# Loading the first FFN weights in pieces of the contraction, with six PSUM banks open at once for the first row tile

## The chip, the cores and the metric

The kernel runs on one core of a Trainium2 chip. The metric is the device time of one execution in microseconds (us). The profile's "span", from the first to the last instruction, is about 1.8 us shorter than that time.

## The reference, cut to what matters

A layernorm of `x` (2048 rows of 640) feeds a SwiGLU feed-forward network and an attention over the last 512 cached keys of 32 heads. Only the start of the feed-forward part is touched by the change:

```python
xn = layernorm(x)                    # 2048 x 640
g = silu(xn @ w_gate)                # 640 x 1536
u = xn @ w_up                        # 640 x 1536
ffn = (g * u) @ w_down
out = x + attention(xn) * silu(ffn)
```

## The kernel before

The rows are handled in tiles of 128. The first four row tiles go through the first three column blocks of the hidden layer one at a time, as soon as their data is there; everything after that uses matmuls of 512 columns. The first columns of both weight matrices (384 columns, 480 KB each) are loaded whole, between the first row tiles of `x`. SP and ACT name the issuing queues of SyncE and ScalarE.

```python
load_x(0)                       # halves: one by SP, one by ACT
load_x(1, nc.scalar)
load_gu(0, nc.scalar)           # gate by SP, up by ACT, all 5 chunks of the contraction
load_x(2); load_x(3)            # SP
load_gu(1)
# ... cut: x tiles 4 to 7, the other weights

def ln_stats(t, between=None):  # VectorE: two bn_stats, between() after the first, bn_aggr
def ln_sqrt(t):                 # ScalarE: Sqrt of the variance
def ln_apply(t):                # VectorE: reciprocal, then (x - mean) * rstd -> xn
def ready(t):
    ln_transpose(t)             # TensorE: 5 transposes of xn into PSUM
    # ... cut: ScalarE (tile 0: part by VectorE) copies them to xnT
    if t < 3:
        ln_sqrt(t + 1)
    if t == 2:
        nc.scalar.activation(act_t[:], one_t[:], ACT.Silu)   # loads the Silu table early

ln_stats(0); ln_sqrt(0)
ln_stats(1, lambda: ln_apply(0))
ready(0)
keep_warm(4)                    # matmuls on zeros
for t in range(4):
    rows = slice(t * P, (t + 1) * P)
    order = [(f, s) for s in range(2) for f in range(3)]      # s: 0 gate, 1 up
    for k, (f, s) in enumerate(order if t == 0 else sorted(order)):
        if k == 4 and t < 3:
            if t < 2:
                ln_stats(t + 2, lambda: ln_apply(t + 1))
            else:
                ln_apply(t + 1)
            ready(t + 1)
        hidden_mm(first[f][s][:, rows], s, f, rows)           # 5 matmuls, one per chunk c
        # ... cut: gates in tile 3
```

The softmax here doesn't subtract the row's maximum and nothing guards it: scores larger than these inputs give would overflow.

## Time and profile before

| | before |
|---|---|
| time, median of 6 runs | 930.38 us (930.01 to 930.88) |
| span of the profiled run | 928.8 us |
| TensorE (PE) busy | 920.7 us, 99% of the span |
| first hidden matmul | 7.66 us |
| first matmul of row tiles 1, 2, 3 | 10.70, 13.04, 15.38 us |
| first 512-column matmul | 17.05 us |

These are lines of the page of the kernel before. They are the span, the busy time of each engine, and the start of the chain that ended last with its shares by engine.

```profile
span 928.8 us, 18808 instructions
PE 920.7 (99%) x8026; PEld 578.7 (62%) x8026; DVE 579.7 (62%) x846; ACT 476.2 (51%) x849; POOL 65.1 (7%) x57
PE 98%; DMA 1%; DVE 1%; ACT 0%; issue 0%; SPq 0%; DVEq 0%
```

TensorE is busy nearly throughout, so only its idle time can be won. The Trainium skill ("Perfetto Trace Analysis", section "Identifying the Most-Contended Engine") warns that matmul busy time is no measure of distance to the roofline. Here it is used for something else: to see where TensorE waits. Those waits sit at the start, as the table by windows of the kernel before shows. Its columns are the stretch and its length, then busy time and instruction count of PE, weight loads (PEld), DVE, ACT and POOL, then clock, DMA share and GB/s.

```profile
0.00:17.05 17.05, 14.05 (x156) 9.76 (x157) 7.42 (x25) 7.26 (x14) 0.79 (x8) 1.00 0.93 280
17.05:928.00 910.95, 906.63 (x7874) 568.95 (x7871) 572.25 (x822) 468.96 (x836) 64.29 (x49) 1.00 0.38 79
```

Of the first 17.05 us TensorE idles 3.00 (17.05 - 14.05). The next two fences are from the timeline of the kernel before. The columns are start, duration of the group, engine, line, operation, output and inputs, shapes, count, and in brackets the idle time before it and what ended it. First TensorE:

```profile
7.66 0.73 PE L271 MATMUL sc<-xnT,wg_sb 128*128 128x128 bf16 x10 [0.58 <-DMA wg_sb<-in_B_w_gate_dram]
9.47 0.45 PE L259 MATMUL tp<-ident,xn 128*128 128x128 bf16 x5 [0.52 <-DVE xn L248]
10.70 0.44 PE L271 MATMUL sc<-xnT,wg_sb 128*128 128x128 bf16 x5 [0.22 <-ACT xnT L321]
```

Then VectorE (DVE):

```profile
8.37 0.49 DVE L225 BATCH_NORM_STATS2 stats<-x_t 128x6 f32<-128x320 bf16 x1 [1.32 <-DMA x_t<-in_A_x_dram]
8.78 0.15 DVE L247 RECIPROCAL rstd<-rstd 128x1 f32<-128x1 f32 x1
8.96 0.45 DVE L248 TENSOR_SCALAR xn<-x_t,mv,rstd 128x640 bf16<-128x640 bf16 x1
```

The statistics at 8.37 are those of x tile 2. They wait 1.32 us for their DMA. The reciprocal and the `TENSOR_SCALAR` behind them make xn of row tile 1, which needs nothing of x tile 2; it is only queued behind. TensorE's transposes of tile 1 at 9.47 wait for that xn. In the chain of waits of the kernel before this DMA is the one large early piece (columns: start, length, what):

```profile
2.24 6.11 DMA x_t<-in_A_x_dram
8.37 0.49 DVE stats L225
```

### The profile page before, as it was taken

The numbers are of one execution on the slowest core, as the hardware profiler recorded it, in microseconds if no ns is written. First come the engines' busy times: TensorE is split into PE (matmuls) and PEld (weight loads), VectorE is DVE, ScalarE is ACT, GpSimd is POOL, SyncE is SP. The second block draws the span as 40 slices with busy tenths as digits, with TensorE's granted clock in tenths as the row PEclk, the third lists the DMA queues.
The fourth block names the chain that finished last, engine by engine and source line by source line (L and its number), as shares of the span: only waits on it lengthen the run. The fifth ranks groups of instructions, "written<-read, shape, count | busy, mean of one in ns | idle before, by whom it ended". The sixth has DMA issues, their size and how long they took to land.

```text
span 928.8 us, 18808 instructions
## 1 busy us (share of the span) xinstructions
PE 920.7 (99%) x8026; PEld 578.7 (62%) x8026; DVE 579.7 (62%) x846; ACT 476.2 (51%) x849; POOL 65.1 (7%) x57
## 2 busy tenths in 40 slices
PE   8999999999999999999999999999999999999997
PEld 5455555574847475757575757575666666666675
DVE  5433321467676767676766667676767676767656
ACT  3222222556565656565555555555555555656561
POOL 0000000000000000000000000000000000003975
PEclk9999999999999999999999999999999999999999
DMA  9321510053535343343434342525252616262523
GB/s 299 69 43 44 114 35 1 1 80 85 93 71 87 77 80 84 73 91 73 91 69 95 60 104 56 108 52 112 41 123 38 126 35 129 34 144 61 147 59 107
DMA packets 240084, 76.34 MB, mean 82 GB/s; under 512 B 221056, under 2 KB 240000, under 8 KB 240000
## 3 DMA queue, kind: packets, MB, share of 16 engines
q1 hardware_dynamic: 239120, 74.40, 38.1%
q8 instruction: 63, 1.03, 0.5%
q10 hardware_dynamic: 880, 0.74, 0.3%
q14 instruction: 21, 0.17, 0.1%
HBM read 39.45 MB, written 2.62 MB: 45 GB/s over the span
## 4 chain that ended last, share of the span: by engine, by line
PE 98%; DMA 1%; DVE 1%; ACT 0%; issue 0%; SPq 0%; DVEq 0%
PE sc L497 22%; PE mm L414 22%; PE mm L450 18%; PE sc L428 18%; PE sc L271 10%; PE mm L293 6%; DMA x_t<-in_A_x_dram 1%; PE sc L450 1%; PE mm L306 0%; PE mm L271 0%; ACT xnT L321 0%; DVE s_f L540 0%; PE mm L428 0%; ACT L327 0%; DVE ob L538 0%
## 5 line engine op out<-in xcount | busy, mean ns | idle before, releaser
L432 ACT ACTIVATE p_t<-sc 128x1024 bf16<-128x1024 f32 x254 | 253.1, 1023 | 136.4 <-PE sc L428 136.4
L419 DVE TENSOR_REDUCE qT<-mm 128x512 bf16<-128x1024 f32 x189 | 231.3, 1224 | 104.0 <-PE mm L414 101.5
L467 ACT ACTIVATE O_b<-mm,r 128x192 bf16<-128x192 f32 x484 | 164.5, 422 | 175.2 <-DVE r L456 97.6
L414 PE MATMUL mm<-xnT,wq_p 64*128 64x512 bf16 x1890 | 235.0, 376 | 0.0
L497 PE MATMUL sc<-wo_p,OT_b 128*128 128x320 bf16 x1482 | 223.4, 299 | 0.0
L512 DVE TENSOR_TENSOR sacc<-sacc,sc 128x640 f32<-128x640 f32 x216 | 176.7, 821 | 60.9 <-PE sc L497 60.9
L428 PE MATMUL sc<-qT,khat 64*128 64x512 bf16 x1524 | 195.5, 376 | 0.0
L450 PE MATMUL mm<-V_p,p_t 128*128 128x193 bf16 x1984 | 185.8, 246 | 0.0
L450 PEld LDWEIGHTS <-p_t 128*128 128x128 bf16 x2048 | 173.1, 97 | 14.9 <-issue 7.0
L497 PEld LDWEIGHTS <-OT_b 128*128 128x128 bf16 x1488 | 143.5, 98 | 47.3
L414 PEld LDWEIGHTS <-wq_p 64*128 64x128 bf16 x1890 | 90.7, 94 | 112.4 <-issue 4.2
L428 PEld LDWEIGHTS <-khat 64*128 64x128 bf16 x1536 | 74.8, 94 | 91.0
L279 DVE TENSOR_TENSOR hT<-sc,sg 128x512 bf16<-128x512 f32 x46 | 31.7, 692 | 85.8 <-ACT sg L278 85.8
L515 POOL TENSOR_TENSOR sacc<-sacc,g_76 128x640 f32<-128x640 f32 x16 | 22.1, 1402 | 757.8 <-ACT O_b L467 757.8
L456 DVE RECIPROCAL r<-mm 128x4 f32<-128x4 f32 x124 | 22.7, 183 | 73.1 <-PE mm L450 68.9
L278 ACT ACTIVATE sg<-sc 128x512 bf16<-128x512 f32 x46 | 27.4, 597 | 73.2 <-PE sc L271 71.6
L271 PE MATMUL sc<-xnT,wg_sb 128*128 128x512 bf16 (+1 forms) x260 | 58.0, 354 | 1.2 <-ACT xnT L321 0.7
L271 PE MATMUL sc<-xnT,wu_sb 128*128 128x512 bf16 (+1 forms) x260 | 58.2, 354 | 0.0
L293 PE MATMUL mm<-wd_sb,hT 128*128 128x320 bf16 x384 | 56.6, 299 | 0.0
L293 PEld LDWEIGHTS <-hT 128*128 128x128 bf16 x384 | 37.6, 98 | 18.9
L271 PEld LDWEIGHTS <-wu_sb 128*128 128x128 bf16 x285 | 25.8, 98 | 26.5
L271 PEld LDWEIGHTS <-wg_sb 128*128 128x128 bf16 x285 | 25.8, 98 | 24.7 <-DMA wg_sb<-in_B_w_gate_dram 1.1
(63 smaller groups left out, 250.5 us busy)
## 6 DMA issues: line engine op xcount, KB each, us to landing
wo_p<-in_A_wo_dram SPq DMA_DIRECT2D x16, 480.0 KB, 4.3
K_p<-in_A_k_cache_dram SPq DMA_DIRECT2D x32, 192.0 KB, 3.3
V_p<-in_A_v_cache_dram SPq DMA_DIRECT2D x32, 192.0 KB, 3.1
wq_p<-in_A_wq_dram SPq DMA_DIRECT2D x64, 80.0 KB, 3.1
wq_p<-in_A_wq_dram SPq DMA_DIRECT2D x16, 160.0 KB, 3.3
x_r<-in_A_x_dram SPq DMA_DIRECT2D x16, 160.0 KB, 4.1
x_t<-in_A_x_dram SPq DMA_DIRECT2D x14, 160.0 KB, 3.1
wg_sb<-in_B_w_gate_dram SPq DMA_DIRECT2D x4, 480.0 KB, 6.7
```

The source lines that it names most:

```text
L271: nc.tensor.matmul(out, w_sb[:, c, f * P : (f + 1) * P], xnT[:, c, qc], start=(c == 0), stop=(c == NC - 1),)
L278: nc.scalar.activation(sg[:], g, ACT.Silu)
L279: nc.vector.tensor_tensor(hTs[b][:, f, :], u, sg[:], ALU.mult)
L293: nc.tensor.matmul(dn[:, 0:HD], hTs[b][:, f, ti * P : (ti + 1) * P], wd_sb[:, f, cols], start=(f == 0), stop=(f == NF - 1),)
L414: nc.tensor.matmul(q_ps[:, h, :], pairs[pr]["wq"][r, c, j * P : (j + 1) * P], xnT[r, c, b * 512 : (b + 1) * 512], start=(c == 0), stop=(c ...
L419: nc.vector.reduce_sum(qTs[i][:, j, :], q_ps[:, :, :].rearrange("p h n -> p n h"), axis=AX.X)
L428: nc.tensor.matmul(sc[:, h, :], khat[r, j, ks], qT[r, j, :], start=(j == 0), stop=(j == 2))
L432: nc.scalar.activation(p_t[:, :, :], sc[:, :, :], ACT.Exp, scale=scale)
L450: nc.tensor.matmul(acc[:, k, h * 256 : h * 256 + Dh + 1], Ps[i][kc][:, h, qt * P : (qt + 1) * P], V_p[:, kc, h, 0 : Dh + 1], start=(kc == ...
L467: nc.scalar.activation(O_b[:, qt, h, :], a_k[:, h, 0:Dh], ACT.Copy, scale=r[:, k, h, :])
L497: nc.tensor.matmul(ps, OTs[i][:, 3 * qt + j, :], pairs[i // NB]["wo"][:, j, n * HD : (n + 1) * HD], start=(first and j == 0), stop=(end an ...
L512: nc.vector.tensor_tensor(s_t, s_t, sc[:, :, 0:HD], ALU.add)
```

## The change

The intent is to let TensorE begin on row tile 0 when the first chunk of the contraction has landed, instead of waiting for a whole matrix. The first gate and up weights are each loaded as three DMAs (1, 2 and 2 chunks of 128 rows). The contraction is the sum over the 640 features of a row, five chunks of 128. Row tile 0 runs chunk by chunk over all six accumulators, so six banks of PSUM, the memory in which TensorE accumulates, are open at once. The diff does more than its title says: it also takes the statistics of x tile 2 out of the way of tile 1's normalization, places the next tile's transposes after three of six groups instead of four, moves the Silu table load behind tile 3's copy, and drops one of the warm-up matmuls.

```diff
-        load_gu(0, nc.scalar)
+        for cs in (slice(0, 1), slice(1, 3), slice(3, NC)):
+            for eng, w_sb, w in ((nc.sync, wg_sb, B_w_gate), (nc.scalar, wu_sb, B_w_up)):
+                src = w[cs.start * P : cs.stop * P, 0:FQ].rearrange("(c p) f -> p c f", p=P)
+                eng.dma_start(out=w_sb[:, cs, 0:FQ], in_=src)
         load_x(2)
         load_x(3)
 ...                                              # hidden_mm takes the chunks to do, cs
         def ready(t):
 ...
-            if t < 3:
-                ln_sqrt(t + 1)
-            if t == 2:
-                nc.scalar.activation(act_t[:], one_t[:], ACT.Silu)
 ...
         ready(0)
-        keep_warm(4)
+        ln_sqrt(1)
+        keep_warm(3)
+        banks = [(f, s) for f in range(3) for s in range(2)]
         for t in range(4):
-            order = [(f, s) for s in range(2) for f in range(3)]
-            for k, (f, s) in enumerate(order if t == 0 else sorted(order)):
-                if k == 4 and t < 3:
-                    if t < 2:
-                        ln_stats(t + 2, lambda: ln_apply(t + 1))
+            order = [(*fs, [c]) for c in range(NC) for fs in banks]
+            if t:
+                order = [(*fs, range(NC)) for fs in banks]
+            for k, (f, s, cs) in enumerate(order):
+                if k == len(order) * 3 // 5 and t < 3:
+                    if t == 1:
+                        ln_stats(3, lambda: ln_apply(2))
                     else:
                         ln_apply(t + 1)
                     ready(t + 1)
-                hidden_mm(first[f][s][:, rows], s, f, rows)
+                    if t == 0:
+                        ln_stats(2)
+                    if t < 2:
+                        ln_sqrt(t + 2)
+                    else:
+                        nc.scalar.activation(act_t[:], one_t[:], ACT.Silu)
+                hidden_mm(first[f][s][:, rows], s, f, rows, cs)
```

More of the change, by code (lines that the diff above doesn't have):

```diff
@@ L186, in load_x, with load_gu @@
                 eng.dma_start(out=x_t[t][:], in_=x2[t * P : (t + 1) * P, :])
-        def load_gu(q, eng=nc.sync):
+        def load_gu(q):
             cols = slice(q * FQ, (q + 1) * FQ)
@@ L192, in load_gu @@
             )
-            eng.dma_start(
+            nc.sync.dma_start(
                 out=wu_sb[:, :, cols], in_=B_w_up[:, cols].rearrange("(c p) f -> p c f", p=P)
@@ L266, with hidden_mm @@
         hTs = {}
-        def hidden_mm(out, s, f, qc):
+        def hidden_mm(out, s, f, qc, cs=range(NC)):
             w_sb = (wg_sb, wu_sb)[s]
-            for c in range(NC):
+            for c in cs:
                 nc.tensor.matmul(
@@ L319, in ready @@
             ln_transpose(t)
-            rows, n = slice(t * P, (t + 1) * P), 3 if t == 0 else NC
+            rows = slice(t * P, (t + 1) * P)
+            n = NC if t else 3
             nc.scalar.copy(xnT[:, 0:n, rows], tps[t][:, 0:n, :])
```

## The prediction

> **What bounds the kernel now.** The page gives PE 920.7 us busy of 928.8 us (99%); the chain that ended last is 98% PE. The change touches only the time before the first 512-column matmul (17.05 us in the timeline); from there to 40 us PE is busy 22.95 of 22.95 us (table by windows). So only PE's idle time before 17 us can be won, and a gain there should shift everything behind it.
>
> **That stretch before (timeline, waits, chain).** 120 hidden matmuls and 15 transposes from 7.66 to 17.05 us, at 0.28 us per five: 7.6 us of work in 9.4 us. Losses:
> - PE waits 0.58 us for the first gate weights (7.08 to 7.66).
> - Tile 1's transposes start at 9.47 (0.52 us idle): its xn is computed on VectorE behind a stats instruction that waits for x tile 2 (it begins at 8.37). This DMA is the chain's largest early piece (6.1 us).
> - From a tile's transposes to the next tile's first matmul pass 1.23 us (transposes, 0.69 us copy); only two groups (0.56 us) fill it; tiles cost 2.34 us each (10.70, 13.04, 15.38).
> - The table load (1.28 us) stands before tile 3's copy.
>
> **What changes.**
> 1. Weights in three pieces per matrix, contraction-major order; same bytes and queue order. X tile 2 and the last up piece should land near 8.3 as now, the first pieces near 5 to 6, the middle near 7.3 (estimate from the DMA view's bytes per us, landing about 1 us after the bytes). PE starts near 7.1 and does 18 of 30 matmuls before the last pieces.
> 2. Tile 1's normalization no longer waits for x tile 2: transposes near 8.15.
> 3. Transposes after 3 of 6 groups instead of 4: a tile costs about 2.1 us (0.84 + 1.23).
> 4. The Silu table load moves behind tile 3's copy; the gates start near 15.5 (16.13 now), early enough.
> 5. Cost: four more DMA issues of 0.45 to 0.6 us, two on ScalarE's queue ahead of the Sqrt table load (2.43 to about 3.5), so the first Sqrt slips 0.3 us (4.69 to 5.0), and tile 0's copies with it. The Trainium skill, "DMA: Bandwidth & Descriptors", section "Rules for kernel authors", says that issuing engines share the same 16 DMA engines; the overlapping landings here agree, so I count no bandwidth gain.
>
> **Sum.** Tile 0 starts at 7.1, tile 1 9.4, tile 2 11.9 (held by x tile 2's statistics), tile 3 14.1, first 512-column matmul 15.8 instead of 17.05. All 1.2 us lie on the critical path: 930.39 - 1.2 = 929.2 us.
>
> **Range** 928.4 to 930.1. Within 2% is practically certain: all idle before 17 us is under 4 us.
>
> **What shows each step.** Timeline: first hidden matmul near 7.1, released by the xnT copy, not the weights; tile 1's transposes near 8.2, before x tile 2's stats end; tile starts as above; Sqrt table load near 3.5; at most about 0.4 us gap before tile 2's transposes. PE's busy total nearly unchanged, its idle 1.2 us less.
>
> **What would make it wrong.** Issue on ScalarE slower than 0.6 us each: every 0.1 us delays tile 0. Pieces landing late through uneven sharing between the queues: tile 0 stalls within the contraction. A later clock rise (the warm-up matmuls take 427 ns each until about 6 us): up to 1 us. The late table load delaying the first gate until a PSUM bank is missing: I expect over 1 us of slack.

## The result, and the profile after

The changed kernel takes 929.82 us (median of 6 runs, 929.58 to 929.89) against 930.38 us: a gain of 0.56 us. A later set of five runs gave 929.95 against 930.45, a gain of 0.50 us. The ratio is 0.9993 with a 95% interval of 0.998 to 1.0006. Ratios here are the mean time of one kernel's fast runs over that of the other's in the same rounds, so they are not quite the ratio of the medians. By this measure the two kernels are the same; the traces and the experiments are needed to say more. In the first set all six runs of the changed kernel (929.89 at most) lie below all six of the kernel before (930.01 at least); in the later set the ranges overlap.

The page after, the lines that answer to those of before:

```profile
span 927.8 us, 18795 instructions
PE 919.5 (99%) x8009; PEld 578.7 (62%) x8025; DVE 579.4 (62%) x846; ACT 475.5 (51%) x849; POOL 65.0 (7%) x57
```

In this trace the span is 1.0 us shorter. The busy total of PE fell by 1.2 us, but it is of little use here: 17 fewer matmul records are in it, while the change removes one matmul. The table by windows, cut at the first 512-column matmul of the kernel after, is clearer:

```profile
0.00:16.00 16.00, 13.77 (x155) 9.78 (x156) 7.17 (x24) 6.60 (x13) 0.79 (x8) 1.00 0.91 278
```

TensorE idles 2.23 us there (16.00 - 13.77) instead of 3.00. The 1.05 us by which the 512-column matmuls start earlier are 0.77 us of idle time and 0.28 us of work, about the one warm-up matmul. The timeline of TensorE after:

```profile
7.06 0.22 PE L274 MATMUL sc<-xnT,wg_sb 128*128 128x128 bf16 x1
8.09 0.44 PE L262 MATMUL tp<-ident,xn 128*128 128x128 bf16 x5
9.31 0.44 PE L274 MATMUL sc<-xnT,wg_sb 128*128 128x128 bf16 x5
10.98 0.45 PE L262 MATMUL tp<-ident,xn 128*128 128x128 bf16 x5 [0.67 <-DVE xn L251]
16.00 0.38 PE L274 MATMUL mm<-xnT,wg_sb 128*128 128x512 bf16 x1
```

Tile 0 starts at 7.06 without a wait, tile 1's transposes come at 8.09 instead of 9.47, and tile 1 starts at 9.31 instead of 10.70: 1.39 us won. Then a new wait stands at 10.98, where the transposes of tile 2 wait 0.67 us for their xn. The timeline of VectorE after shows why:

```profile
7.44 0.45 DVE L251 TENSOR_SCALAR xn<-x_t,mv,rstd 128x640 bf16<-128x640 bf16 x1
8.79 0.89 DVE L228 BATCH_NORM_STATS2 stats<-x_t 128x6 f32<-128x320 bf16 x2 [0.90 <-DMA x_t<-in_A_x_dram]
10.48 0.45 DVE L251 TENSOR_SCALAR xn<-x_t,mv,rstd 128x640 bf16<-128x640 bf16 x1
```

Tile 1's xn (7.44) is no longer behind the statistics of x tile 2. But x tile 2 lands at 8.76 now, 0.4 us later than in the trace of before, and from there its statistics, its square root and its xn (10.48) set the pace. Tiles 1 to 2 take 2.90 us instead of 2.34, tiles 2 to 3 take 2.12 instead of 2.34. The sum is -1.39 + 0.56 - 0.22 = -1.05 us. The chain of waits after agrees; the same DMA is still its large early piece, but now it leads to tile 2:

```profile
3.42 5.34 DMA x_t<-in_A_x_dram
8.79 0.90 DVE stats L228 x2
```

**Does a gain at the start reach the end?** Yes, and completely. For all 14 traces (two of the kernel before, two of the changed one, ten of other versions) the span is the start of the first 512-column matmul plus 911.75 to 911.91 us. That start ranges from 15.62 to 17.73 us. So nothing is given back later, and a difference in time is a difference before about 17 us. It also means that single traces scatter: the second trace of the changed kernel has that start at 16.31 instead of 16.00, and medians of several runs are needed for the size of an effect.

**From x tile 2 to the 512-column matmuls.** The table of the experiments below allows one more difference: the start of the first 512-column matmul minus the start of x tile 2's statistics. It is 8.67 to 8.68 us in both traces of the kernel before and in e2 (old order of VectorE's work), 8.23 in e8 (only the wait put back), and 7.21 to 7.23 in both traces of the changed kernel, both of e1, in e9 and in e10. So the new order shortens the path behind x tile 2 by 1.46 us, 1.02 us of it by the one move that e8 undoes; how late x tile 2 lands then adds to the time. In e3, e5 and e7 (7.50, 7.87, 8.02) a weight load that TensorE waits for in tile 0 is what holds instead; in e4 (7.39) the table load adds 0.18.

### The profile page after: what moved, and what is told of

Its sections match the earlier page's. It is cut to its first block, busy times and chain, and to the rows that moved or that the text cites. A ratio compares the mean times of both kernels' runs of the same rounds, so it can differ in the third digit from the quotient of the medians.

```text
span 927.8 us, 18795 instructions
## 1 busy us (share of the span) xinstructions
PE 919.5 (99%) x8009; PEld 578.7 (62%) x8025; DVE 579.4 (62%) x846; ACT 475.5 (51%) x849; POOL 65.0 (7%) x57
## 4 chain that ended last, share of the span: by engine, by line
PE 98%; DMA 1%; DVE 1%; issue 0%; DVEq 0%
PE sc L508 22%; PE mm L425 22%; PE mm L461 18%; PE sc L439 18%; PE sc L274 10%; PE mm L296 6%; DMA x_t<-in_A_x_dram 1%; PE sc L461 1%; PE mm L274 0%; PE mm L309 0%; DVE s_f L551 0%; PE mm L439 0%; DVE stats L228 0%; DVE ob L549 0%; DVE s_f L548 0%
```

## The experiments

Theory A: the gain comes from taking tile 1's normalization off the wait for x tile 2, with a smaller part from the earlier transposes; the pieces themselves add nothing and make x tile 2 land later. Theory B, the change's own intent: the pieces and the contraction-major order bring the gain. The expectations call them by these letters. Each kernel was run on the same chip as runs of the kernel before; all gave correct results. The edits below are cut, and are against the changed kernel; only that of e2 is against the kernel before. "Start" is the start of the first 512-column matmul in the one profiled run.

| version | time, median (range) | minus before, same chip | start | x tile 2's statistics begin |
|---|---|---|---|---|
| before_again | 930.72 (930.09 to 930.99) | +0.18 | 17.07 | 8.40 |
| after_again | 929.95 (929.33 to 930.27) | -0.50 | 16.31 | 9.10 |
| e1_reorder_only | 928.99 (928.90 to 930.16) | -1.46 | 16.59 | 9.38 |
| e1_again | 929.03 (928.92 to 929.32) | -1.51 | 15.62 | 8.39 |
| e2_pieces_only | 930.86 (930.59 to 931.39) | +0.41 | 17.73 | 9.06 |
| e3_x2_early | 929.39 (928.86 to 929.60) | -1.06 | 15.77 | 8.27 |
| e4_table_before_copy | 929.86 (929.76 to 930.28) | -0.68 | 16.60 | 9.21 |
| e5_after_four | 930.25 (929.94 to 930.79) | -0.34 | 16.70 | 8.83 |
| e7_gates_both | 929.15 (928.48 to 929.39) | -1.39 | 15.69 | 7.67 |
| e8_wait_back | 930.57 (930.32 to 930.96) | -0.02 | 17.34 | 9.11 |
| e9_issue_late | 929.38 (929.26 to 930.54) | -1.21 | 15.69 | 8.48 |
| e10_x2_behind_ups | 929.47 (929.03 to 930.39) | -1.12 | 16.62 | 9.40 |

The intervals of the ratios are about 0.0012 wide to each side, or 1.1 us. The single runs say more: all five runs of e1_again, for example, lie below every run of the kernel before on that chip (929.32 at most against 930.09 at least).

### after_again and before_again: both kernels once more

No edit.

> The changed kernel once more, as the yardstick of the runs beside it. Both theories: the trace repeats (tile 0's first hidden matmul 7.1 us, tile 1's 9.3, tile 2's 12.2, tile 3's 14.3, first 512-column matmul 16.0). If the 1.05 us that the first trace shows before 17 us survive to the end, the timed gain over the kernel before is about 1.0 us (929.4); if some of it is given back later, about 0.5 us.

> The kernel before itself, for a second trace. The six traces so far agree that the span is the start of the first 512-column matmul plus 911.8 us (911.75 to 911.83), so the spread of the times (930.0 to 931.0) should be the spread of that start. Theory A and B alike: the start is near 16.8 (from the median time) rather than the 17.05 of the first trace, the sum holds again within 0.1 us, and x tile 2 and the whole gate weights land at times that differ by some tenths of a us from the first trace though the bytes moved by 7 us are the same.

The gain of after_again was 0.50 us, as in the first set, so the expectation's alternative "some of it is given back later" had the right number for the wrong reason. The sum of start and 911.8 us held. The first pair of traces had simply caught a slow run of the kernel before (930.71 us) and a quick one of the changed kernel (929.60). The trace of before_again was again one with a start of 17.07, and not the 16.8 that the median suggests. Its landings did not scatter as expected: its gates landed at 7.64 and x tile 2 at 8.38, as in the first trace.

### e1_reorder_only and e1_again: the reordering without the pieces

```diff
-        for cs in (slice(0, 1), slice(1, 3), slice(3, NC)):   # six DMAs
+        for eng, w_sb, w in ((nc.sync, wg_sb, B_w_gate), (nc.scalar, wu_sb, B_w_up)):
+            src = w[:, 0:FQ].rearrange("(c p) f -> p c f", p=P)
+            eng.dma_start(out=w_sb[:, :, 0:FQ], in_=src)
-            order = [(*fs, [c]) for c in range(NC) for fs in banks]
+            order = [(f, s, range(NC)) for s in range(2) for f in range(3)]
```

> The changed kernel with the first weights loaded whole and gates before ups in tile 0, as before; the reordering of VectorE and ScalarE work and the transposes after 3 of 6 groups stay. Theory A (the gain comes from taking tile 1's normalization off the wait for x tile 2 and from earlier transposes; the pieces add nothing and make x tile 2 land later): x tile 2 lands near 8.35 again, tile 0 starts 7.66, tile 1 9.7, tile 2 11.9, tile 3 14.1, first 512-column matmul 15.8, so 0.2 us EARLIER than the changed kernel. Theory B (the pieces and the contraction-major order bring the gain): first 512-column matmul at 16.5 or later, since PE again waits 0.58 us for whole weights.

> The reordering without the pieces once more: the profiled run of the first time was the slowest of its five (930.16 against 928.9 to 929.7), with gates landing at 8.42. Theory A: the median is again near 929.0, 0.8 us below the changed kernel's 929.8; if the profiled run is a quick one, gates land near 7.6, tile 0 starts near 7.5, tile 2's transposes wait little and the first 512-column matmul starts near 15.4. Theory B (the pieces help, the first median was luck): median near 930.

Without the pieces the kernel is faster still: 928.99 and 929.03 us, a gain of 1.46 and 1.51 us over the kernel before, where the changed kernel has 0.50 to 0.56. (Beside it on one chip: 928.90 to 930.16 against 929.33 to 930.27, so single runs overlap.) Theory B falls. The first profiled run was the slowest of its five (930.16), with a late landing of the gates (8.42), and its start of 16.59 alone would have spoken for theory B. The profiled run of e1_again was the slowest of its five too (929.32), but only 0.3 us above their median. TensorE's timeline of it:

```profile
7.66 0.73 PE L273 MATMUL sc<-xnT,wg_sb 128*128 128x128 bf16 x10 [0.92 <-DMA wg_sb<-in_B_w_gate_dram]
8.51 0.44 PE L261 MATMUL tp<-ident,xn 128*128 128x128 bf16 x5
9.73 0.44 PE L273 MATMUL sc<-xnT,wg_sb 128*128 128x128 bf16 x5
10.61 0.45 PE L261 MATMUL tp<-ident,xn 128*128 128x128 bf16 x5
```

And VectorE's:

```profile
7.04 0.45 DVE L250 TENSOR_SCALAR xn<-x_t,mv,rstd 128x640 bf16<-128x640 bf16 x1
8.39 0.89 DVE L227 BATCH_NORM_STATS2 stats<-x_t 128x6 f32<-128x320 bf16 x2 [0.91 <-DMA x_t<-in_A_x_dram]
```

This pairs with the trace of before_again: tile 0 starts at 7.66 and 7.65, x tile 2's statistics at 8.39 and 8.40. So what TensorE gets from memory is the same, and the 1.45 us between the starts (17.07 and 15.62) are the reordering alone. TensorE still waits 0.92 us for the gates. With whole gates in hand it does 15 matmuls, then the transposes of tile 1 at 8.51, whose xn was ready at 7.5. The chain of waits of this trace begins with the gates (landed at 7.61), yet earlier gates alone would win almost nothing: tile 2's transposes start at 10.61, and their xn, which hangs on x tile 2, was ready only at 10.55. Tile 1 starts 1.0 us earlier than in before_again (9.73 against 10.73), and each of the next two tiles takes 2.11 us instead of 2.34.

### e2_pieces_only: the pieces without the reordering

```diff
-        load_gu(0, nc.scalar)
+        # the six DMAs of the change
-            order = [(f, s) for s in range(2) for f in range(3)]
+            order = [(*fs, [c]) for c in range(NC) for fs in banks]     # tile 0
-                if k == 4 and t < 3:
+                if k == len(order) * 2 // 3 and t < 3:
```

> The kernel before with only the weights in pieces and the contraction-major order in tile 0; the order of VectorE's and ScalarE's work is as before. Theory A: tile 0 starts near 7.1 but gains nothing, because tile 1's transposes still stand behind x tile 2, which now lands at 8.76: transposes near 9.9, tile 1 11.1, tile 2 13.5, tile 3 15.8, first 512-column matmul 17.4 to 17.5, that is 0.4 us LATER than the kernel before. Theory B: first 512-column matmul at 16.5 or earlier.

The pieces alone gained nothing: the median is 0.41 us higher (930.86), but the ranges overlap (930.59 to 931.39 against 930.17 to 931.00 and one run of 933.48), so the times alone do not show a loss. The trace, of the slowest of the five runs, shows the expected course: tile 0 starts early, and tile 1's transposes stand behind x tile 2 all the same. VectorE and TensorE in the timeline of e2_pieces_only:

```profile
9.06 0.49 DVE L228 BATCH_NORM_STATS2 stats<-x_t 128x6 f32<-128x320 bf16 x1 [1.71 <-DMA x_t<-in_A_x_dram]
9.65 0.45 DVE L251 TENSOR_SCALAR xn<-x_t,mv,rstd 128x640 bf16<-128x640 bf16 x1
10.15 0.45 PE L262 MATMUL tp<-ident,xn 128*128 128x128 bf16 x5 [0.56 <-DVE xn L251]
```

X tile 2 began 0.66 us later than in before_again (9.06 against 8.40), and the start of the 512-column matmuls is 0.66 us later too (17.73 against 17.07).

### e8_wait_back: the wait put back, all else as changed

```diff
-                    if t == 1:
-                        ln_stats(3, lambda: ln_apply(2))
+                    if t < 2:
+                        ln_stats(t + 2, lambda: ln_apply(t + 1))
-                    if t == 0:
-                        ln_stats(2)
```

> The changed kernel with one thing undone: in tile 0 the statistics of x tile 2 stand again ahead of tile 1's normalization on VectorE. Theory A (this wait is the main loss that the change removes): x tile 2 lands near 9.0, tile 1's transposes slip from 8.1 to 8.6 to about 10.1, tile 1 starts 11.3, tile 2 13.4, tile 3 15.5, first 512-column matmul 17.1 to 17.2, time 930.8, about 1 us above the changed kernel: no gain over the kernel before is left. Theory B: less than 0.3 us lost.

With the statistics of x tile 2 ahead of tile 1's xn again, nothing of the gain is left (930.57 against 930.59 for the kernel before). VectorE waits 1.92 us for x tile 2, and TensorE in the timeline of e8_wait_back idles 1.70 us ahead of tile 1's transposes:

```profile
9.11 0.49 DVE L228 BATCH_NORM_STATS2 stats<-x_t 128x6 f32<-128x320 bf16 x1 [1.92 <-DMA x_t<-in_A_x_dram]
10.21 0.45 PE L262 MATMUL tp<-ident,xn 128*128 128x128 bf16 x5 [1.70 <-DVE xn L251]
```

This is the sharpest test of the cause, since one reordering of VectorE's queue was undone and the pieces, the contraction-major order, the earlier transposes and the dropped warm-up matmul all stayed. The changed kernel itself was not run on this chip; its gains of 0.56 and 0.50 us come from other sets.

### e3_x2_early: x tile 2 ahead of the third piece

```diff
         for cs in (slice(0, 1), slice(1, 3), slice(3, NC)):
+            if cs.start == 3:
+                load_x(2)
 ...
-        load_x(2)
```

> The changed kernel with x tile 2 issued ahead of the third gate piece instead of after it. Theory A: x tile 2 lands near 7.5 instead of 8.76, its statistics follow tile 1's normalization without a wait, tile 2's transposes start near 10.4 instead of 10.98 and everything behind them moves up: tile 2 11.6, tile 3 13.7, first 512-column matmul 15.4 instead of 16.0. The third pieces land later by up to 0.4 us, hidden behind tile 1's transposes and copy. Theory B (weights bound): the later third pieces stall tile 0 and the first 512-column matmul is not earlier than 16.0.

The time fell to 929.39, 0.56 us below after_again on the same chip, so x tile 2 is what holds the changed kernel. The size agrees with the expectation (0.6 us); the landings do not quite. X tile 2 lands at 8.25 and not near 7.5, tile 2's transposes stand at 10.75 and not 10.4, and the third gate piece lands at 9.16, so that TensorE waits for it (0.34 us, timeline of e3_x2_early):

```profile
9.21 0.23 PE L275 MATMUL sc<-xnT,wg_sb 128*128 128x128 bf16 x1 [0.34 <-DMA wg_sb<-in_B_w_gate_dram]
```

### e4_table_before_copy: the table load in its old place

```diff
+                    if t == 2:
+                        nc.scalar.activation(act_t[:], one_t[:], ACT.Silu)   # ahead of ready(3)
 ...
-                    else:
-                        nc.scalar.activation(act_t[:], one_t[:], ACT.Silu)
```

> The changed kernel with the Silu table load put back ahead of tile 3's copy. If the table load's place matters by itself: it starts right after tile 3's Sqrt, holds tile 3's copy back by 0.2 to 0.4 us, tile 3's transposes to its first matmul take 1.5 us instead of 1.23, and the time is 0.3 us above the changed kernel's (930.1). If it is hidden, as a rival reading of the earlier copy wait has it, the interval stays 1.23 us and the time 929.8.

In the timeline of e4_table_before_copy the load does hold the copy, which starts 0.2 us later than it could (0.49 us after the transposes at 13.52 would be 14.01):

```profile
12.80 1.28 ACT L345 ACT_TABLE_LOAD   x1
14.20 0.68 ACT L325 COPY xnT<-tp 128x640 bf16<-128x640 bf16 x1
```

From tile 3's transposes (13.52) to its first matmul (14.93) pass 1.41 us instead of 1.24, so its place is worth 0.17 us in the trace. The medians (929.86; the changed kernel 929.82 and 929.95, on other chips) do not resolve that.

### e5_after_four: transposes after four of six groups

```diff
-                if k == len(order) * 3 // 5 and t < 3:
+                if k == len(order) * 2 // 3 and t < 3:
```

> The changed kernel with the next tile's transposes after 4 of 6 groups again (20 of 30 matmuls in tile 0). My sum: tiles 1 to 2 are held by x tile 2's statistics in any case, so only tile 2 to tile 3 grows, from 2.11 to 2.34 us: the time 0.2 us above the changed kernel (930.05). If the position costs on every tile, 0.5 us or more.

Tile 2 to tile 3 takes 2.33 us instead of 2.12 (12.70 to 15.03), as expected, and ScalarE's copy is what TensorE waits for once more (timeline of e5_after_four):

```profile
15.03 0.44 PE L274 MATMUL sc<-xnT,wg_sb 128*128 128x128 bf16 x5 [0.22 <-ACT xnT L325]
```

The gain over the kernel before on the same chip is 0.34 us, 0.16 to 0.22 less than the changed kernel's, near the 0.2 expected. In the trace tile 0 waited for up pieces as well (0.57 us for two of them), and the transposes after 20 matmuls came behind that wait. One trace doesn't tell how often that happens.

### e9_issue_late: is it the later issue that makes x tile 2 late?

The three gate DMAs keep SP's queue busy for 1.79 us instead of 0.80, so x tile 2 is issued at 3.42 instead of 2.24. The timelines of SP's queue, before:

```profile
1.38 0.80 SPq L190 DMA_DIRECT2D wg_sb<-in_B_w_gate_dram  x1
2.24 0.99 SPq L186 DMA_DIRECT2D x_t<-in_A_x_dram  x2
```

and after:

```profile
1.38 1.79 SPq L202 DMA_DIRECT2D wg_sb<-in_B_w_gate_dram  x3
3.42 1.87 SPq L186 DMA_DIRECT2D x_t<-in_A_x_dram  x2
```

The experiment is e1 with two loads of one row each ahead of x tile 2:

```diff
+        spare = lnx.tile([1, 2, D], bf, name="spare", bufs=1)
+        for r in range(2):
+            nc.sync.dma_start(out=spare[:, r, :], in_=x2[r : r + 1, :])
         load_x(2)
```

> The reordering with whole weights, and two loads of one row (1.25 KB each) issued ahead of x tile 2, so that its issue slips by about 0.9 us, as the pieces make it slip by 1.2, with next to no bytes added. If x tile 2 lands later in the piece versions because it is issued later: it lands near 9.0 here too and the first 512-column matmul is 0.4 us later than 15.6, time 929.4. If its landing follows from the bytes ahead of it in the queue and the pieces slow those bytes down: it lands at 8.4 and the time stays 929.0.

The issue moved to 2.96, 0.7 us and not 0.9. X tile 2's statistics began at 8.48, within 0.1 us of the versions with whole weights. In this trace the later issue did not make x tile 2 late. The median is 929.38, though, as the other alternative had it, and two of its five runs took 930.1 and 930.5; the profiled run had its first rows of x late as well, so the median doesn't decide it. Total bytes don't explain it either: by 7.0 us SP's queue had moved 0.69 MB and ACT's 0.68 in the first trace of before, 0.75 and 0.72 in after_again, and yet x tile 2 landed at 8.35 in the one and 9.07 in the other. What makes it land later with pieces stays open.

### e7_gates_both and e10_x2_behind_ups: looking for a better version

The reordering is kept, the gates are fetched first by both queues, and the ups are split over both. In e7 x tile 2 is issued ahead of the ups, in e10 behind the first part of them.

```diff
-        # the six DMAs of the change
+        load_part(wg_sb, B_w_gate, nc.sync, slice(0, 3))
+        load_part(wg_sb, B_w_gate, nc.scalar, slice(3, NC))
+        load_x(2)                                              # e10: behind the next line but one
+        load_part(wu_sb, B_w_up, nc.sync, slice(0, 2))
+        load_part(wu_sb, B_w_up, nc.scalar, slice(2, NC))
-            order = [(*fs, [c]) for c in range(NC) for fs in banks]
+            order = [(f, s, range(NC)) for s in range(2) for f in range(3)]
```

> A version built from the findings: the reordering kept, gates before ups in tile 0, the gate weights fetched first by both queues (three chunks on one, two on the other), x tile 2 next, then the ups split over both queues. Theory A with bytes deciding the landings: gates land near 6.6, tile 0 starts at 6.9, x tile 2 lands near 7.3 and no longer holds tile 2, ups land near 8.3 and stall tile 0 a little; tile 1 9.1, tile 2 11.2, tile 3 13.4, first 512-column matmul 15.1, time 928.7, 0.3 us below the reordering alone. If more, smaller issues make everything land later, as the changed kernel's pieces seem to do, the time is no better than the reordering alone (929.0 or more).

> The version with gates fetched by both queues, but x tile 2 behind the first part of the ups instead of ahead of it. If queue position decides the landing: ups land near 8.4 instead of 8.88, x tile 2 near 8.6 instead of 7.6; tile 1 starts 9.2 instead of 9.7, tile 2 about 11.7 (held by x tile 2's statistics), first 512-column matmul 15.5, time 929.0, within noise of the reordering alone (929.0). If x tile 2 lands at 9.0 or later, as in the piece versions: 16.0 and 929.5.

In e7 TensorE starts tile 0 at 6.86 and x tile 2 is there in time, but the ups arrive late (timeline of e7_gates_both):

```profile
8.88 0.85 PE L278 MATMUL sc<-xnT,wu_sb 128*128 128x128 bf16 x10 [0.59 <-DMA wu_sb<-in_B_w_up_dram]
```

Its median of 929.15 is no better than the reordering alone (928.99 and 929.03), its quickest run is (928.48 against 928.90). In e10 the profiled run was the slowest of its five (930.39): the gates landed near 7.6, the last part of the ups near 9.1, and x tile 2's statistics began at 9.40. Its median of 929.47 fits the alternative in the expectation, but the trace is not that of an ordinary run. Neither beats e1, which is also the simplest edit; e1 beats both kernels.

## Why the prediction was right or wrong

The measured 929.82 us lies in the range of 928.4 to 930.1, and the two times are within 2% of each other, as was said. The range is 1.7 us wide and takes in e1, e3, e4 and the changed kernel alike, so the number alone says little about the mechanism. The forecast gain of 1.2 us is about double the measured one (0.50 to 0.56 us by medians, 1.05 us between the first two traces).

- **Bound and reach: right.** Only the first 17 us count, and a gain there moves everything behind it. The span minus the start of the 512-column matmuls is the same within 0.16 us in 14 traces.
- **Tile 0 and tile 1: right.** 7.06 and 9.31 us were measured against 7.1 and 9.4 predicted, and the transposes of tile 1 at 8.09 against 8.15. The second trace had tile 1 at 9.87, with a stall for an up piece that had been expected at 7.3 and released TensorE at 8.02.
- **The step that failed is item 1: "X tile 2 and the last up piece should land near 8.3 as now."** With pieces x tile 2's statistics began at 8.79, 9.06, 9.10, 9.21, 8.83 and 9.11 in the six traces that keep this queue order, 9.0 on average; with whole weights at 8.37, 8.40, 8.39, 8.48 and once 9.38 (e10, with the loads split over both queues, had 9.40). The reasoning behind it, same bytes and same queue order give the same landing, is what the runs contradict. Since tile 2 is held by exactly this landing in the changed kernel, the delay comes out of the gain: 1.46 to 1.51 us without the pieces, 0.50 to 0.56 with them. The traces show a delay of about 0.6 us (0.4 with the late one counted); the medians would need about 0.95 (an estimate: 1.46 less 0.5). That the traces of before and of e1 are of runs slower than their medians (930.71, 930.72, 930.16, 929.32) fits this, but does not prove it.
- **Where the gain comes from: half right.** Item 2 (the wait for x tile 2) carries it, as e1 and e8 show. I counted the pieces as a second gain through the earlier start of tile 0; the earlier start is real (0.6 us), but TensorE then waits at tile 2. That the total still came out on the right side is luck in this respect: one move outweighed what the pieces cost.
- **Transposes after three groups: right.** 2.12 us per tile where nothing else holds it, against 2.34.
- **Table load: right in direction.** Its place is worth 0.17 us in a trace, and the gates start at 15.70 (predicted 15.5) without holding TensorE.
- **Cost on ScalarE's queue: smaller than said, with a different path.** The first Sqrt started at 4.85 us and not 5.0. Tile 0's transposes still slipped by 0.27 us in the first trace, mostly because the reciprocal on VectorE stood behind the statistics of x tile 1, which waited for their own DMA until 4.95; in e2, e4 and e5 it did wait 0.17 to 0.28 us for the Sqrt.
- **"Its idle 1.2 us less": wrong as written.** In the traces idle time before the 512-column matmuls fell by 0.77 us; the rest of the 1.05 us is the warm-up matmul that was dropped. The drop was not tested by itself, but e8 keeps it and gains nothing.

## What to carry to other kernels

When a change bundles a new load pattern with a new instruction order, test the two apart: here the order alone was worth about 1.5 us, the pieces that give the change its name took two thirds of it away, and the bundle looked like a small success. Before splitting a load so that an engine can start earlier, look for what that engine waits for next; here an instruction on VectorE that waited for data of a later tile held up the tile behind it in the queue, and moving it back cost nothing that a trace shows. For effects below 1 us, compare medians of several runs and take from traces only intervals within one trace, since x tile 2 of the same load pattern was in use at 8.37 us in one run and at 9.38 in another.

## What the Trainium skill lacked or had wrong

- "DMA: Bandwidth & Descriptors", sections "Anatomy of one DMA — SWDGE (gpsimd) path" and "Issuing engines are not separate DMA queues": the first gives a DMA as a fixed 2 us plus bytes, for GpSimd's path, and the second says that the time to initiate a DMA is usually small relative to the DMA itself. The second agrees with the gates of the kernel before (0.80 us of issuing from 1.38, landed at 7.65). What the page lacks is how far the landing of one load spreads from run to run: the same 480 KB load of the gates, issued at 1.38 us, landed at 7.65 and at 8.42 us (e1_reorder_only), and x tile 2's statistics began at 8.37 and 9.38, with the same bytes moved by 7.0 us (0.69 and 0.68 MB per queue in both). Nor does it say how the issuing time grows when one load is cut in pieces: SP's queue was taken 1.79 us by the three gate pieces, 0.80 us by the whole load.
- "TensorE: Matmul & The Clock Gate", section "Back-to-back issue gap": it states about 81 ns per matmul for streams of weight load and matmul at 128 columns, and about 131 ns at 512. Here tile 3 runs 30 such pairs of 128 columns in 1.67 us (14.33 to 16.00), 56 ns each, and five of 512 columns take 1.08 us, 216 ns each. Both match its figures for the isolated gap instead.
- "ScalarE: Activation LUTs", section "What ACT_TABLE_LOAD costs": its 1283 ns for the load agree (1.28 us at 13.20 in the kernel before), but no drain of 1380 ns was seen with it: the load began 0.02 us after the Sqrt before it had ended (13.18), and the next activation at 14.49, 0.01 us after the load's end.
